# A spectral mixer and a token MLP on one core: the second product behind the up projection, PSUM read two banks at a time, and one operand loaded in K tile pairs

## The chip, the cores and the metric

The kernel runs on one core of one Trainium2 chip. The metric is the device time of one execution in microseconds (us). TensorE (PE) multiplies, VectorE (DVE) and ScalarE (ACT) prepare operands and read PSUM, SyncE (SP) issues most loads, GpSimd (POOL) issues most stores. PSUM has room for eight results of 128x512 floats, called banks here.

## The reference

```python
g = sigmoid((x * gate_w).sum(-1, keepdims=True))          # x: 2048 x 1024
a = x @ Wd_re.T ; b = x @ Wd_im.T                         # hidden DFT
A = Ws_re @ a - Ws_im @ b                                 # sequence DFT, real part
h = layernorm(x)                                          # over the 1024 channels
u = gelu(h.T @ w1 + b1)                                   # 1024 x 3584
B = (u @ w2 + b2).T                                       # 2048 x 1024
return g * A + (1 - g) * B
```

All values are 32-bit floats. The order of the two DFT products is free, so the kernel multiplies the sequence matrix first.

## The kernel before, in words

There are four matrix products, called stages: **q** (class `Fourier`: sequence transform of x), **y** (class `Mixed`: the second product, q with the hidden matrix, scaled by the gate and stored to the output), **u** (class `Up`: normalised x with w1, then gelu) and **o** (class `Down`: u with w2, added onto the output). Each stage is a product of 4x4 blocks by 4x2 blocks, done by a fixed scheme in 26 block products where the plain way has 32 (`SCHEME`). Each of the 26 multiplies a signed sum of blocks of one side by a signed sum of blocks of the other. The stationary operand (128x128 at a time) is called W and the moving one (128x512 at a time) R.

One block product runs over K tiles of 128 rows (four in q, y and u, seven in o). For every K tile both sums are made by DVE additions (`add`, `sub`), and each operand is split in two parts (`split_into`: ACT writes the high part, DVE the remainder, called lo). For each bank PE then issues three matmuls: hi·hi, hi·lo and lo·hi (lines 902 to 904). The K tiles are taken in groups (`takes`: 1, 1, 2 in q means one tile, one tile, then two together); a group does all its matmuls into the first bank, then all into the second, and so on. A product fills `nm * nn` banks: 8 in q, 4 in y, 7 in u, 4 in o.

After the last group of a product its banks are read: for each output block that the scheme names, one instruction per bank copies (L938 on ACT, L940 on DVE) or adds (L946, DVE alone) the bank into an accumulator tile (`q_c`, `y_c`, `u_c`, `o_c`). Where two products that follow each other feed nearly the same outputs, the second goes on adding in the same banks; it is then called chained, and its first matmul into a bank must wait until the reads of that bank are done.

SBUF is 51 tiles of 128x1024 and one half tile. A planner in the kernel (`Graph`) gives every task a due time from the PE order, hands out tiles and banks, and writes the order of each engine's instructions once and for all; PE's own order is the order in which the stages are built. The loads of x for the row sums, the squares and the normalisation are tasks of that planner too, with their place given by `SUMS_AT`, `SQUARES_AT` and `H_LEAD`.

Of the kernel before, what the change touches and what calls it, by code (L numbers as in the profile page):

```python
# [14 lines left out]
P = 128  # L15
S = 2048
D = 1024
# [7 lines left out]
SLOTS = {"f": 51, "h": 1, "ps": 8}  # L25
LATE = 3.0

# [112 lines left out]
Q_GAP = 8  # L140
U_ORDER = [20, 9, 8, 19, 15, 18, 1, 16, 10, 4, 21, 22, 11, 7, 3, 17, 5, 14, 23, 6, 24, 0, 13, 12, 2, 25]
# [68 lines left out]
SUMS_AT, SUMS_STEP = ("q", 12), 2.5  # L210
SQUARES_AT, SQUARES_STEP = ("y", 6), 2
H_LEAD, H_EACH = 25, 1.3
# [49 lines left out]
class Buf:  # L262
    def __init__(self, kind, name, t=None, parts=1, dtype=F32):
        self.kind, self.name, self.t, self.parts, self.dtype = kind, name, t, parts, dtype
        self.writer = [None] * parts
        self.readers = [[] for _ in range(parts)]
        self.taker = None
        self.users, self.opens = set(), False


class View:
# [8 lines left out]
    def reg(self):  # L280
        return (self.buf, self.part)

# [19 lines left out]
class Store:  # L302


    def __init__(self, slots):
        self.free = {k: [Slot(k, i) for i in range(n)] for k, n in slots.items()}
        self.part = {F32: [], F32R: []}

    def pairs(self, ahead):
        return sum((max(0, ahead[d] - len(self.part[d])) + 1) // 2 for d in self.part)  # L310

    def fits(self, b, ahead):
        if b.kind != "h":
            return len(self.free[b.kind]) > ahead[b.kind]
        if len(self.part[b.dtype]) > ahead[b.dtype]:
            return True
        return len(self.free["f"]) + len(self.free["h"]) > ahead["f"] + self.pairs(ahead)

    def take(self, b):
        if b.kind != "h":  # L320
# [3 lines left out]
        halves = self.part[b.dtype]  # L324
# [3 lines left out]
        else:  # L328
            pool = self.free["h"] or self.free["f"]
            b.slot, b.opens = (min(pool, key=lambda s: s.at), 0), True  # L330
            pool.remove(b.slot[0])
            if b.slot[0].pool == "f":
# [3 lines left out]
    def give(self, b, now):  # L336
        s, h = b.slot
        s.at = now
        if h is not None and s.pool == "f":
            s.inside[h] = False  # L340
            if s.inside[1 - h]:
                self.part[b.dtype].append(b.slot)
                return
            self.part[b.dtype].remove((s, 1 - h))
# [3 lines left out]
class Graph:  # L348
# [63 lines left out]
    def schedule(self):  # L412
        store = Store(SLOTS)
        waiting = {k: [] for k in ("f", F32, F32R, "ps")}
# [11 lines left out]
        for t in self.tasks:  # L426
# [3 lines left out]
            for b in t.need:  # L430
                insort(waiting[b.dtype if b.kind == "h" else b.kind], t)
# [14 lines left out]
        def start(t, e):  # L446
# [3 lines left out]
            for b in t.need:  # L450
                store.take(b)
                waiting[b.dtype if b.kind == "h" else b.kind].remove(t)
# [50 lines left out]
def gated_mix_kernel(  # L503
# [30 lines left out]
        "ps": (ctx.enter_context(tc.tile_pool(name="psum", bufs=1, space=bass.MemoryType.PSUM)), H),  # L534
# [138 lines left out]
    class Bilinear:  # L673
# [10 lines left out]
        behind = ()  # L684
        ahead = 3
# [723 lines left out]
```

## Time and profile before

| | |
|---|---|
| time, median of 3 runs | 1849.24 us (1849.20 to 1850.03) |
| span of the profiled execution (first to last instruction) | 1847.2 us |
| what the median has beside that span | 2.0 us |
| PE busy | 1843.0 us, 8130 matmuls |
| DVE busy | 1692.7 us, 2372 instructions |
| ACT busy | 876.2 us, 1311 instructions |
| DMA moved | 472.71 MB, mean 256 GB/s |

The profiled execution's own time is not given apart from its span. The span is cut by the stages' first matmuls: q begins at 4.06 us, y at 570.55, u at 853.43, o at 1348.47, and the last matmul ends at 1843.74. A busy PE is not by itself a PE at its peak, so the distance between the starts of matmuls is what to read, and the waits that PE had.

### The profile page before, as it was taken

Reading aid. Unit: us, or ns where it says so; the run is one execution under the profiler, and the core shown is the slowest. Engines: PE = TensorE matmul, PEld = TensorE weight load, DVE = VectorE, ACT = ScalarE, POOL = GpSimd, SP = SyncE. Lnnn points to the kernel's source line nnn. Section 1 sums busy time; section 2 is a strip of 40 time slices with the busy share of each in tenths; the row PEclk is TensorE's granted clock in tenths of the full one; section 3 lists DMA queues with packets and bytes.
Section 4 is the critical chain, followed back from the end, with each engine's and each line's share of the span. In section 5 each row is a group of like instructions: output and inputs, shape, how many; then the busy total and the mean of one; then the engine's idle time right before and its main releaser. Section 6 shows DMA issues by size and latency. Waiting matters only on the chain.

```text
span 1847.2 us, 24030 instructions
## 1 busy us (share of the span) xinstructions
PE 1843.0 (100%) x8130; PEld 1525.2 (83%) x8130; DVE 1692.7 (92%) x2372; ACT 876.2 (47%) x1311; POOL 207.2 (11%) x355
## 2 busy tenths in 40 slices
PE   9999999999999999999999999999999999999999
PEld 7888888888888888888888888888888888888887
DVE  8999679989989999999789698879999999999995
ACT  5533334534344686597343344444654534444441
POOL 0100010111021001001121000001220000001111
PEclk9999999999999999999999999999999999999999
DMA  9977377969698888988676547667899676775963
GB/s 377 368 260 270 126 280 289 349 236 376 237 333 313 303 292 273 332 312 292 219 256 241 174 136 255 225 210 247 301 365 295 193 210 208 217 215 128 301 156 69
DMA packets 189739, 472.71 MB, mean 256 GB/s; under 512 B 23152, under 2 KB 23920, under 8 KB 189616
## 3 DMA queue, kind: packets, MB, share of 16 engines
q1 hardware_dynamic: 156384, 368.40, 58.4%
q0 software_dynamic: 32944, 102.52, 16.6%
q8 instruction: 63, 1.03, 0.2%
q14 instruction: 60, 0.49, 0.1%
q10 hardware_dynamic: 288, 0.26, 0.0%
HBM read 367.29 MB, written 103.81 MB: 255 GB/s over the span
## 4 chain that ended last, share of the span: by engine, by line
PE 100%; DVE 0%; issue 0%; DVEq 0%
PE ps_q_p L902 10%; PE ps_q_p L904 10%; PE ps_q_p L903 10%; PE ps_u_p L904 9%; PE ps_u_p L902 9%; PE ps_u_p L903 9%; PE ps_o_p L902 9%; PE ps_o_p L904 9%; PE ps_o_p L903 9%; PE ps_y_p L903 5%; PE ps_y_p L904 5%; PE ps_y_p L902 5%; PE ps_q_p L1049 0%; PE ps_q_p L1026 0%; PE pw L1343 0%; DVE o_c L946 0%
## 5 line engine op out<-in xcount | busy, mean ns | idle before, releaser
L904 PE MATMUL ps_q_p<-q_p_r_hi,q_p_w_lo 128*128 128x512 f32 x728 | 283.2, 389 | 0.0
L902 PE MATMUL ps_o_p<-o_p_r,o_p_w 128*128 128x512 f32 x726 | 282.4, 389 | 0.0
L903 PE MATMUL ps_o_p<-o_p_r,o_p_w 128*128 128x512 f32 x726 | 282.4, 389 | 0.0
L904 PE MATMUL ps_o_p<-o_p_r,o_p_w 128*128 128x512 f32 x726 | 282.4, 389 | 0.0
L903 PE MATMUL ps_u_p<-u_p_r_lo,u_p_w_hi 128*128 128x512 f32 x588 | 228.7, 389 | 0.0
L902 PE MATMUL ps_q_p<-q_p_r_hi,q_p_w_lo 128*128 128x512 f32 x584 | 227.2, 389 | 0.0
L903 PE MATMUL ps_q_p<-q_p_r_lo,q_p_w_lo 128*128 128x512 f32 x584 | 227.2, 389 | 0.0
L902 PE MATMUL ps_u_p<-u_p_r_lo,u_p_w_hi 128*128 128x512 f32 x504 | 196.1, 389 | 0.0
L904 PE MATMUL ps_u_p<-u_p_r_lo,u_p_w_lo 128*128 128x512 f32 x504 | 196.1, 389 | 0.0
L599 ACT ACTIVATE q_p_r_hi<-q_R_p 128x1024 fp32r<-128x1024 f32 (+1 forms) x100 | 104.2, 1053 | 161.8 <-DVE q_R_p L569 78.7
L599 ACT ACTIVATE u_p_w_hi<-u_W_p 128x896 fp32r<-128x896 f32 x104 | 97.1, 950 | 141.1 <-DVE u_W_p L569 69.5
L904 PEld LDWEIGHTS ps_q_p<-q_p_r_hi,q_p_w_lo 128*128 128x128 f32 x728 | 136.7, 188 | 28.4
L904 PEld LDWEIGHTS ps_o_p<-o_p_r,o_p_w 128*128 128x128 f32 x726 | 136.3, 188 | 28.4
L902 PEld LDWEIGHTS ps_o_p<-o_p_r,o_p_w 128*128 128x128 f32 x726 | 136.3, 188 | 28.2
L903 PEld LDWEIGHTS ps_o_p<-o_p_r,o_p_w 128*128 128x128 f32 x726 | 136.3, 188 | 28.2
L599 ACT ACTIVATE o_p_r<-o_R_p 128x512 fp32r<-128x512 f32 x117 | 72.5, 626 | 120.9 <-PE ps_o_p L904 37.3
L903 PEld LDWEIGHTS ps_u_p<-u_p_r_lo,u_p_w_hi 128*128 128x128 f32 x588 | 110.4, 188 | 23.0
L903 PEld LDWEIGHTS ps_q_p<-q_p_r_lo,q_p_w_lo 128*128 128x128 f32 x584 | 109.6, 188 | 22.7
L902 PEld LDWEIGHTS ps_q_p<-q_p_r_hi,q_p_w_lo 128*128 128x128 f32 x584 | 109.7, 188 | 22.6
L946 DVE SCALAR_TENSOR_TENSOR q_c<-ps_q_p,q_c 128x512 f32<-128x512 f32 x168 | 110.3, 686 | 15.6 <-PE ps_q_p L904 11.5
L606 DVE TENSOR_TENSOR q_p_r_lo<-q_R_p,q_p_r_hi 128x1024 fp32r<-128x1024 f32 (+1 forms) x100 | 120.4, 1215 | 4.5 <-ACT q_p_r_hi L599 4.4
L904 PEld LDWEIGHTS ps_u_p<-u_p_r_lo,u_p_w_lo 128*128 128x128 f32 x504 | 94.6, 188 | 19.6
(322 smaller groups left out, 3989.4 us busy)
## 6 DMA issues: line engine op xcount, KB each, us to landing
q_R_p<-in_ct_dram SPq DMA_DIRECT2D x131, 512.0 KB, 7.5
u_W_p<-in_w_dram SPq DMA_DIRECT2D x120, 448.0 KB, 4.7
o_R_p<-in_w_dram SPq DMA_DIRECT2D x99, 256.0 KB, 4.7
o_R_p<-u SPq DMA_DIRECT2D x83, 256.0 KB, 5.2
q<-q_c POOLq DMA_DIRECT2D x80, 256.0 KB, 6.2
o_W_p<-in_w_dram SPq DMA_DIRECT2D x76, 256.0 KB, 4.9
q_W_p<-in_x_dram SPq DMA_DIRECT2D x75, 256.0 KB, 5.5
u<-u_c POOLq DMA_DIRECT2D x72, 256.0 KB, 4.7
```

The costliest lines, as they stand in the source:

```text
L599: g.add({"ACT": act(v.n)}, key, lambda e: nc.scalar.activation(hi.ap, v.ap, AF.Copy, scale=-1.0 if negate else 1.0), r=(v.reg,), w=(hi.reg,))
L606: nc.vector.tensor_sub(lo.ap, v.ap, hi.ap.bitcast(F32))
L902: nc.tensor.matmul(bank.ap, wh.ap[:, c], rh.ap[:, e], start=a, stop=False, skip_group_check=True)
L903: nc.tensor.matmul(bank.ap, wh.ap[:, c], rl.ap[:, e], start=False, stop=False, skip_group_check=True)
L904: nc.tensor.matmul(bank.ap, wl.ap[:, c], rh.ap[:, e], start=False, stop=b, skip_group_check=True)
L946: lambda e: nc.vector.scalar_tensor_tensor(o.ap, ps.ap, scale, o.ap, op0=ALU.mult, op1=ALU.add),
```

## The change

The change does seven things.

1. The stages are built in the order q, u, y, o (before: q, y, u, o).
2. In q, u and y PSUM is handed out as four pairs of banks, and one instruction of 1024 columns reads a pair (`banks`, `take`). In u the seventh bank of a product is still single; o keeps single banks (`together = False`). A pair is read when its second bank is complete. The loop over a product's banks now has n outside and m inside.
3. In q the stationary operand is handled in tiles of two K tiles (`Q_WIDE = "W"`: 128x1024 in place of two of 128x512), and the K tiles are taken 2, 2 (`Q_TAKES`). The first product of q alone takes 1, 1, 2.
4. The row sums start at product 4 of q (before: 12), the squares at product 12 of q (before: product 6 of y), and the normalisation begins 8 steps before use (before: 25); a step is one K tile of a product.
5. The product of x with the gate weights moves from the row sums into the normalisation, with a scratch tile of its own; the gate's last steps move to product 10 of u.
6. The planner counts at most seven earlier claims when it decides whether a task may take a tile (`RESERVE`).
7. A method `strassen`, which would do one product of q by seven half-size products, and its two helper classes are added. It is called for the products listed in `Q_INNER`, and that list is empty.

```diff
-SLOTS = {"f": 51, "h": 1, "ps": 8}
+SLOTS = {"f": 51, "h": 1, "pp": 4}
+RESERVE = 7
...
+Q_DMA = {}
+Q_INNER = ()
...
-SUMS_AT, SUMS_STEP = ("q", 12), 2.5
-SQUARES_AT, SQUARES_STEP = ("y", 6), 2
-H_LEAD, H_EACH = 25, 1.3
+SUMS_AT, SUMS_STEP = ("q", 4), 2.5
+SQUARES_AT, SQUARES_STEP = ("q", 12), 2
+GATES_AT = "u", 10
+H_LEAD, H_EACH = 8, 0.6
...
-Q_TAKES = 1, 1, 2
+Q_TAKES = 2, 2
...
-Q_WIDE, Y_WIDE, O_WIDE = "", "WR", ""
+Q_WIDE, Y_WIDE, O_WIDE = "W", "WR", ""
...
-                if not store.fits(b, {k: bisect_left(waiting[k], t) for k in waiting}):
+                if not store.fits(b, {k: min(bisect_left(waiting[k], t), RESERVE) for k in waiting}):
...
+                if j in self.inner:
+                    self.strassen(j, factor)
+                    continue
...
-            for m in range(self.nm):
-                c = slice(m * P, (m + 1) * P)
-                for n in range(self.nn):
-                    if first:
-                        self.PS[j % self.chains, m, n] = View(Buf("ps", f"ps_{self.name}_p{j}_{m}_{n}", None, 4), 0, H)
+            if first:
+                self.banks(j)
+            for n in range(self.nn):
+                for m in range(self.nm):
+                    c = slice(m * P, (m + 1) * P)
...
+        def banks(self, j):
+            every = [(m, n) for n in range(self.nn) for m in range(self.nm)]
+            for i, (m, n) in enumerate(every):
+                name = f"ps_{self.name}_p{j}_{m}_{n}"
+                if not self.together or i == len(every) - 1 and i % 2 == 0:
+                    self.PS[j % self.chains, m, n] = View(Buf("ps", name, None, 4), 0, H)
+                elif i % 2 == 0:
+                    both = Buf("pp", name, None, 2)
+                    self.PS[j % self.chains, m, n] = View(both, 0, H, 0)
+                else:
+                    self.PS[j % self.chains, m, n] = View(both, H, H, 1)
+
+        def take(self, key, j, m, n, eps):
+
+            bank, at = self.PS[j % self.chains, m, n], [(m, n)]
+            if bank.buf.kind == "pp":
+                if bank.c0 == 0:
+                    return
+                at.insert(0, (m - 1, n))
+                bank = View(bank.buf, 0, D)
...
+        def groups(self, j=None):
+            return super().groups() if j != 0 else [(0,), (1,), (2, 3)]
+
+        def unit(self, x_, k, ks):
+            return ks if x_ in self.wide and len(ks) == 2 else k
...
-        g.add({"DVE": dve(D)}, key, lambda e: nc.vector.scalar_tensor_tensor(
-            v.ap, v.ap, 1.0, GW.ap, op0=ALU.mult, op1=ALU.mult, accum_out=zg.t[:, col]),
-            r=(v.reg, GW.reg), w=(v.reg, zg))
...
+        g.add({"DVE": dve(D)}, key, lambda e: nc.vector.scalar_tensor_tensor(
+            junk.ap, v.ap, 1.0, GW.ap, op0=ALU.mult, op1=ALU.mult, accum_out=zg.t[:, col]),
+            r=(v.reg, GW.reg), w=(junk.reg, zg))
...
-    for st in (Fourier(), Mixed(), Up(), Down()):
+    for st in (Fourier(), Up(), Mixed(), Down()):
```

Three places show how instructions move. In the names, `q_R7_p1_0` is block 7 of R, loaded in product 1 for K tile 0; `_0_1` stands for a pair of K tiles; `_hi` and `_lo` are the two parts of a split; a tile that is used again keeps the name of its first user. What stands in brackets are the queues and engines that an instruction waits for.

The first place is SP at the start of q, the loads behind those of product 0. Before:

```order
L576 DMA q_R7_p1_0_277<-in_ct_dram 128x1024 [waits DMAHW3_49]
L576 DMA q_R4_p1_0_286<-in_ct_dram 128x1024 [waits DMAHW4_49]
L576 DMA q_W1_p0_3_273<-in_x_dram 128x512 [waits DMAHW5_49]
L576 DMA q_W0_p1_0_311<-in_x_dram 128x512 [waits DMAHW6_49]
L576 DMA q_R7_p1_1_315<-in_ct_dram 128x1024 [waits DMAHW7_49]
L576 DMA q_R4_p1_1_333<-in_ct_dram 128x1024 [waits DMAHW0_49]
L576 DMA q_W0_p1_0_311<-in_x_dram 128x512 [waits DMAHW1_49]
L576 DMA q_W0_p1_1_355<-in_x_dram 128x512 [waits DMAHW2_49]
L576 DMA q_R7_p1_2_361<-in_ct_dram 128x1024 [waits DMAHW3_49]
```

and now:

```order
L613 DMA q_R7_p1_0_265<-in_ct_dram 128x1024 [waits DMAHW3_49]
L613 DMA q_R4_p1_0_273<-in_ct_dram 128x1024 [waits DMAHW4_49]
L613 DMA q_R7_p1_1_279<-in_ct_dram 128x1024 [waits DMAHW5_49]
L613 DMA q_R4_p1_1_298<-in_ct_dram 128x1024 [waits DMAHW6_49]
L613 DMA q_W6_p1_0_1_302<-in_x_dram 128x512 [waits DMAHW7_49]
L613 DMA q_W6_p1_0_1_302<-in_x_dram 128x512 [waits DMAHW0_49]
L613 DMA q_W0_p1_0_1_329<-in_x_dram 128x512 [waits DMAHW1_49]
L613 DMA q_W0_p1_0_1_329<-in_x_dram 128x512 [waits DMAHW2_49]
L613 DMA q_W1_p1_0_1_344<-in_x_dram 128x512 [waits DMAHW3_49]
L613 DMA q_W1_p1_0_1_344<-in_x_dram 128x512 [waits DMAHW4_49]
```

Before, the loads of x for the first two K tiles alternated with those of R, 256 KB for each K tile and block. Now both K tiles of three blocks of x (six loads of 256 KB) stand behind the four loads of R of the first two K tiles.

The second place is DVE a little later, where the operands of product 1 are made. Before:

```order
L572 TENSOR_TENSOR q_W0_p1_0_311<-q_W1_p0_3_273,q_W0_p1_0_311 128x512 [waits DMAHW6_49,DMAHW5_49]
L940 TENSOR_SCALAR q_c5_0_410<-ps_q_p0_0_0_282 128x512 [waits PE_49]
L569 TENSOR_TENSOR q_W1_p0_0_257<-q_W0_p1_0_311,q_W1_p0_0_257 128x512 [waits DVE_49]
L606 TENSOR_TENSOR q_p1_r_0_lo_420<-q_R8_p0_0_259,q_p1_r_0_hi_400 128x1024 [waits Activation_49]
L569 TENSOR_TENSOR q_R7_p1_1_315<-q_R7_p1_1_315,q_R4_p1_1_333 128x1024 [waits DMAHW7_49,DMAHW0_49]
L604 SCALAR_TENSOR_TENSOR q_p1_w_0_lo_436<-q_W1_p0_0_257,q_p0_w_1_hi_325 128x512 [waits Activation_49]
L569 TENSOR_TENSOR q_R8_p0_1_264<-q_R7_p1_1_315,q_R8_p0_1_264 128x1024 [waits DVE_49]
L572 TENSOR_TENSOR q_W0_p1_1_355<-q_W0_p1_0_311,q_W0_p1_1_355 128x512 [waits DMAHW2_49,DMAHW1_49]
L940 TENSOR_SCALAR q_c5_4_457<-ps_q_p0_2_0_293 128x512 [waits PE_49]
```

and now:

```order
L606 TENSOR_TENSOR q_R7_p1_0_265<-q_R7_p1_0_265,q_R4_p1_0_273 128x1024 [waits DMAHW4_49,DMAHW3_49]
L606 TENSOR_TENSOR q_R8_p0_0_247<-q_R7_p1_0_265,q_R8_p0_0_247 128x1024 [waits DVE_49]
L606 TENSOR_TENSOR q_R7_p1_1_279<-q_R7_p1_1_279,q_R4_p1_1_298 128x1024 [waits DMAHW6_49,DMAHW5_49]
L643 TENSOR_TENSOR q_p1_r_0_lo_392<-q_R8_p0_0_247,q_p1_r_0_hi_379 128x1024 [waits Activation_49]
L606 TENSOR_TENSOR q_R8_p0_1_252<-q_R7_p1_1_279,q_R8_p0_1_252 128x1024 [waits DVE_49]
L609 TENSOR_TENSOR q_W0_p1_0_1_329<-q_W6_p1_0_1_302,q_W0_p1_0_1_329 128x1024 [waits DMAHW2_49,DMAHW7_49,DMAHW1_49,DMAHW0_49]
L643 TENSOR_TENSOR q_p2_w_0_1_lo_430<-q_W6_p1_0_1_302,q_p2_w_0_1_hi_402 128x1024 [waits Activation_49]
L606 TENSOR_TENSOR q_W1_p1_0_1_344<-q_W0_p1_0_1_329,q_W1_p1_0_1_344 128x1024 [waits DMAHW4_49,DMAHW3_49,DVE_49]
L643 TENSOR_TENSOR q_p1_r_1_lo_447<-q_R8_p0_1_252,q_p1_r_1_hi_418 128x1024 [waits Activation_49]
L606 TENSOR_TENSOR q_R7_p1_2_367<-q_R7_p1_2_367,q_R4_p1_2_371 128x1024 [waits DMAHW6_49,DMAHW5_49]
L641 SCALAR_TENSOR_TENSOR q_p1_w_0_1_lo_462<-q_W1_p1_0_1_344,q_p1_w_0_1_hi_452 128x1024 [waits Activation_49]
```

Before, the operands of K tile 0 (down to the remainder `q_p_w_lo`, line 604) came ahead of most of those of K tile 1. Now the W sums and splits are 1024 wide and hold both K tiles, and the remainder of W for product 1 (line 641) is the eleventh instruction of the piece. Its high part is written by ACT after the addition of line 606 into `q_W1_p1_0_1`.

The third place is DVE in y, at the end of product 9, on which product 10 is chained. Before:

```order
L606 TENSOR_TENSOR y_p12_r_1_5658<-q_W0_p1_3_424,y_p12_r_1_5658 128x512 [waits Activation_49]
L946 SCALAR_TENSOR_TENSOR y_c1_0_5092<-ps_y_p9_0_0_5603,y_c1_0_5092 128x512 [waits PE_49]
L946 SCALAR_TENSOR_TENSOR y_c7_0_5575<-ps_y_p9_0_0_5603,y_c7_0_5575 128x512
L606 TENSOR_TENSOR y_p12_w_1_5679<-y_R4_p4_1_4752,y_p12_w_1_5679 128x512 [waits Activation_49]
L946 SCALAR_TENSOR_TENSOR y_c1_0_5092<-ps_y_p9_1_0_5619,y_c1_0_5092 128x512 [waits PE_49]
L946 SCALAR_TENSOR_TENSOR y_c7_0_5575<-ps_y_p9_1_0_5619,y_c7_0_5575 128x512
L946 SCALAR_TENSOR_TENSOR y_c1_2_5112<-ps_y_p9_2_0_5632,y_c1_2_5112 128x512 [waits PE_49]
L946 SCALAR_TENSOR_TENSOR y_c7_2_5598<-ps_y_p9_2_0_5632,y_c7_2_5598 128x512
L946 SCALAR_TENSOR_TENSOR y_c1_2_5112<-ps_y_p9_3_0_5646,y_c1_2_5112 128x512 [waits PE_49]
L946 SCALAR_TENSOR_TENSOR y_c7_2_5598<-ps_y_p9_3_0_5646,y_c7_2_5598 128x512
```

and now:

```order
L609 TENSOR_TENSOR y_W10_p6_2_3_8658<-y_W10_p6_2_3_8658,y_W10_p11_2_3_9125 128x1024 [waits DMAHW7_49,DMAHW0_49]
L1016 SCALAR_TENSOR_TENSOR y_c1_0_8753<-ps_y_p9_0_0_9211,y_c1_0_8753 128x1024 [waits PE_49]
L1016 SCALAR_TENSOR_TENSOR y_c7_0_9200<-ps_y_p9_0_0_9211,y_c7_0_9200 128x1024
L1016 SCALAR_TENSOR_TENSOR y_c1_2_8775<-ps_y_p9_2_0_9238,y_c1_2_8775 128x1024 [waits PE_49]
L1016 SCALAR_TENSOR_TENSOR y_c7_2_9218<-ps_y_p9_2_0_9238,y_c7_2_9218 128x1024
L643 TENSOR_TENSOR y_p11_r_2_3_lo_9321<-y_R4_p10_2_3_9082,y_p11_r_2_3_hi_9171 128x1024 [waits DMASW5_49]
L641 SCALAR_TENSOR_TENSOR y_p11_w_2_3_lo_9329<-y_W10_p6_2_3_8658,y_p11_w_2_3_hi_9294 128x1024 [waits Activation_49]
```

Before, the eight reads were one for each of four banks and two outputs. Now there are four reads, each of a pair of banks, two for each pair.

More of the change, by code (lines that the diff above doesn't have):

```diff
@@ L413, in schedule @@
         store = Store(SLOTS)
-        waiting = {k: [] for k in ("f", F32, F32R, "ps")}
+        waiting = {k: [] for k in ("f", F32, F32R, "ps", "pp")}
         left, users = {}, {}
@@ L684, in gated_mix_kernel @@
         behind = ()
+        halved = ()
+        together = True
         ahead = 3
@@ L694, in __init__ @@
             small = [r[1] for r in rows]
-            self.again = {j: s for j in range(1, len(rows)) for s in (1, -1) if small[j] == [s * c for c in small[j - 1]]}
+            self.inner = [j for j, r in enumerate(order) if r in self.halved]
+            self.again = {j: s for j in range(1, len(rows)) for s in (1, -1)
+                          if small[j] == [s * c for c in small[j - 1]] and not {j, j - 1} & {*self.inner}}
             self.kept = {}
@@ L711, in __init__ @@
                 opposite = sum(a != -b for a, b in zip(w, v))
-                go_on = min(same, opposite) < sum(a != 0 for a in w)
+                go_on = min(same, opposite) < sum(a != 0 for a in w) and i + n not in self.inner
                 self.chained.append(go_on)
@@ new lines, in take @@
+        def take(self, key, j, m, n, eps):
[5 more added lines that the diff above has]
+                bank = View(bank.buf, 0, D)
+            for q, coef in self.reads[j]:
+                b = self.perm[0][q // 2] * 2 + self.perm[2][q % 2]
+                new, back = (b, m, n) not in self.C, self.back(b, j)
+                if new:
+                    for one in at:
+                        self.C[(b, *one)] = self.c_slots(f"{self.name}_c{b}", b, *one)
+                os = [self.C[(b, *one)] for one in at]
+                o = os[0] if len(at) == 1 else View(os[0].buf, 0, D)
+                if new and back:
+                    for one, part in zip(at, os):
+                        self.bring(key - self.ahead, b, *one, part)
+                if new and not back:
+                    self.copy(key, b, m, n, o, bank, eps * coef)
+                else:
+                    self.accumulate(key, b, m, n, o, bank, eps * coef)
+                if j in self.ends[b]:
+                    for one in at:
+                        self.finish(key + 1, b, *one, self.C.pop((b, *one)), j)
@@ L1032, in matmuls @@
                 return super().matmuls(j, ks, ops, eps)
+            self.banks(0)
             for n in range(2):
[L1034 to L1035 removed]
                 for i, (w, r) in enumerate(((wh, rh), (wl, rh), (wh, rl))):
```

191 lines of the change are left out of this document (146 added, 45 removed).

## The prediction

> **What bounds the kernel now.** I read the page's first two parts, then the waits of PE, then the stages one by one.
>
> ```profile
> span 1847.2 us, 24030 instructions
> PE 1843.0 (100%) x8130; PEld 1525.2 (83%) x8130; DVE 1692.7 (92%) x2372; ACT 876.2 (47%) x1311; POOL 207.2 (11%) x355
> ...
> PEclk9999999999999999999999999999999999999999
> DMA  9977377969698888988676547667899676775963
> ...
> PE 100%; DVE 0%; issue 0%; DVEq 0%
> ```
>
> ```profile
> engine line waited for: us in total, times, longest us
> PE pw L1343 <- PEq L1396: 0.8, 1, 0.8
> ```
>
> The second answer is the whole list of what PE waited for: 0.8 us once, before its warm-up. The chain of waits is PE from end to end. Cut at the stages' borders (q, y, u, o):
>
> ```profile
> 0.00:4.35 4.35, 3.57 (x9) 1.34 (x10) 0.59 (x2) 1.86 (x3) 0.20 (x4) 1.00 0.56 155
> 4.35:570.40 566.05, 566.05 (x2500) 469.06 (x2500) 511.49 (x650) 229.20 (x319) 65.60 (x116) 1.00 0.81 294
> 570.40:853.30 282.90, 282.90 (x1250) 234.33 (x1249) 274.94 (x381) 204.22 (x295) 27.63 (x51) 1.00 0.86 305
> 853.30:1348.60 495.30, 495.30 (x2187) 410.27 (x2186) 435.17 (x575) 224.54 (x323) 64.44 (x119) 1.00 0.67 229
> 1348.60:1843.80 495.20, 495.14 (x2191) 410.17 (x2189) 470.07 (x766) 216.39 (x374) 49.33 (x65) 1.00 0.71 212
> ```
>
> Each row gives the stretch and its length, then busy time and count of PE, weight loads, DVE, ACT and POOL, the granted clock, the DMA share and GB/s. In every stage the length over the matmuls is 0.226 us (566.05/2500, 495.30/2187), at clock 1.00: PE never slows. So the span is about 4.1 us of start, 8100 matmuls at 0.227 us, and 3.4 us after the last matmul; the median has 2.0 us beside it. Only the number of matmuls, their pitch, the two ends, or new stalls can move the time. DVE is behind PE by little (512 of 566, 275 of 283, 435 of 495, 470 of 495 us), but behind.
>
> **What the change leaves alone.** The order of instructions has 8130 matmuls in both programs, since the list of products for `strassen` is empty. Shapes and operand types are the same, so the pitch is. Start-up up to the first matmul and the halved last banks are the same code. A gain could come only from the 7.5 us of both ends, and nothing in the diff touches them: 0.
>
> **Work taken from DVE.** Two durations carry this: rows of several instructions in the order of time (start, length of the row, instruction, count) give the pitch.
>
> ```profile
> 26.74 4.62 DVE L569 TENSOR_TENSOR q_R_p<-q_R_p,q_R_p 128x1024 f32<-128x1024 f32 x4
> ...
> 677.27 3.67 DVE L946 SCALAR_TENSOR_TENSOR y_c<-ps_y_p,y_c 128x512 f32<-128x512 f32 x6
> ```
>
> Six reads of one bank take 3.67 us: 0.60 each, 0.68 for the last with its end. Four of 1024 columns in SBUF take 4.62: 1.13 each, 1.22 for the last. A read of a pair is not in this trace. I take 1.13, by that row; its bounds are 1.13 and twice a single read, 1.20, as the PSUM rows cost what SBUF rows of the same width cost. A pair instead of two banks thus saves 0.07 us. DVE's order is 306 instructions shorter (2358 to 2052). At 0.07 each that is some 20 us, all on an engine for which PE never waited: 0 on the end, bounds 0 and 0. The product with the gate weights (16 x 1.13 = 18 us) moves from q into the end of q and the start of u; u has 60 us of idle DVE to hide it. Without that cover it would cost at most 18 us less the 54 us idle in q: still nothing.
>
> **Loads.** The stretch in which the loads were densest:
>
> ```profile
> 10.00:20.00 10.00, 10.00 (x46) 8.28 (x45) 9.01 (x11) 5.79 (x9) 0.00 (x0) 1.00 1.04 407
> ```
>
> Squares and normalised rows (32 loads of 512 KB, 17 MB) now fall in q: 17 MB over 566 us adds 30 GB/s to 294. That is far under the 407 that were moved here, so they fit: 0. The early ones in y and u go away.
>
> **Stage order.** y no longer follows the stage that makes its input, and o no longer follows u; both gaps grow to a whole stage. u needs only x and the row statistics. What SP, POOL and ACT do is put elsewhere, not added to: 0. If DVE comes late to a border, see the rivals.
>
> **Term 1: product 1 of q starts late.** Before, its first group was one K tile; now it is two, with W in pairs, so the operands of K tile 1 are due 5.4 us earlier. What was there:
>
> ```profile
> 14.99 2.48 DVE L569 TENSOR_TENSOR q_R_p<-q_R_p,q_R_p 128x1024 f32<-128x1024 f32 x2 [0.50 <-DMA q_R_p<-in_ct_dram]
> ...
> 26.55 0.39 PE L902 MATMUL ps_q_p<-q_p_r_hi,q_p_w_hi 128*128 128x512 f32 x1
> 26.77 0.39 PE L903 MATMUL ps_q_p<-q_p_r_lo,q_p_w_hi 128*128 128x512 f32 x1
> 27.00 0.39 PE L904 MATMUL ps_q_p<-q_p_r_hi,q_p_w_lo 128*128 128x512 f32 x1
> ...
> 31.99 0.39 PE L902 MATMUL ps_q_p<-q_p_r_hi,q_p_w_lo 128*128 128x512 f32 x1
> ```
>
> At 407 GB/s 512 KB take 1.29 us. The DVE row waits for block 7 and 4 of K tile 0, landed at 14.9; the same bytes stand ahead of them now. Behind come R for K tile 1 (1 MB: 17.5), then three blocks of x of 512 KB each: 18.8, 20.0, 21.3. DVE goes through the eleven instructions shown of its new order: the first at 14.95; the second waits for the end of the first (16.2); the third for its load (17.5); then 18.65, 19.8, and, no load being late any more, 20.9, 22.05, 23.2, 24.3, 25.45, and the last, the remainder of W, from 26.6 to 27.8. The third matmul wanted it at 27.00. PE stalls **0.9 us** with the signal. Bounds: 0 if loads come a little faster, 2 if one instruction of 1.13 more gets in between. The high part of W comes from ACT after the eighth, at about 26.2, in time. The second group then starts at 26.55 + 0.9 + 10.9 = 38.3; its remainder of W is the ninth instruction after the eleven, 36.8 to 38.0, wanted at 38.8: just in time. Later products have the slack of before.
>
> **Term 2: reads of pairs in y.** y has four banks, so a chained product comes back to a bank after 4 x 6 matmuls. Before, the first bank of product 9's last group was free for reading from 675.27 (six matmuls from 673.91) to 679.35:
>
> ```profile
> 673.91 0.39 PE L902 MATMUL ps_y_p<-y_p_r_hi,y_p_w_hi 128*128 128x512 f32 x1
> ...
> 675.27 0.39 PE L902 MATMUL ps_y_p<-y_p_r_hi,y_p_w_hi 128*128 128x512 f32 x1
> ...
> 679.35 0.39 PE L902 MATMUL ps_y_p<-y_p_r,y_p_w 128*128 128x512 f32 x1
> ...
> 675.47 1.29 DVE L946 SCALAR_TENSOR_TENSOR y_c<-ps_y_p,y_c 128x512 f32<-128x512 f32 x2 [0.79 <-PE ps_y_p L904]
> ...
> 818.07 0.39 PE L902 MATMUL ps_y_p<-y_p_r_hi,y_p_w_hi 128*128 128x512 f32 x1
> ...
> 816.90 1.29 DVE L946 SCALAR_TENSOR_TENSOR y_c<-ps_y_p,y_c 128x512 f32<-128x512 f32 x2
> 818.11 1.22 DVE L606 TENSOR_TENSOR y_p_r_lo<-y_R_p,y_p_r_hi 128x1024 fp32r<-128x1024 f32 x1
> 819.25 3.67 DVE L946 SCALAR_TENSOR_TENSOR y_c<-ps_y_p,y_c 128x512 f32<-128x512 f32 x6
> ```
>
> The window was 4.08 us; two reads began 0.20 after it opened and ended at 676.76, 2.6 us early. A pair is complete only after twelve matmuls and is wanted at the same moment: the window is 2.72 us. One read takes 0.20 + 1.22 and leaves 1.3. Two take 0.20 + 1.13 + 1.22 = 2.55 and leave 0.17. In the changed order two reads of each pair stand before a chained product after products 9, 22 and 24, and after 11 one by ACT and one by DVE, in turn: four places, eight pairs. In thirteen more one read stands. To this comes what DVE is still busy with. The rows bound it: 0 as at 675.47; or, at product 22, 1.0 (its second bank was done 0.20 after 818.07, when the third began, and its reads began at 819.25, behind another instruction). In the middle, 0.5, the first pair of each place stalls 0.5 - 0.17 = 0.33, and the second gains from that stall but for an instruction between them: 0.4 a place, **1.5 us** for four. Bounds: 0, and 8 x (1.0 - 0.17) = 6.6. The thirteen single ones have 1.3 us against 1.0: 0. Behind a waiting read on DVE stand the splits of later products; at 675.47 DVE had waited 0.79 us for PE, so it is ahead of need there and can afford it.
>
> The same reading for q gives a window of 8 x 1.36 - 2.72 = 8.2 us, for u 7 x 1.36 - 2.72 = 6.8 against three reads of 3.7; o keeps single banks. 0 for all three.
>
> **Sum.** The profiled execution: 1847.2 + 0.9 + 1.5 = 1849.6 us of span; with the 2.0 beside it, **1851.6 us**, that is 2.4 more than the median.
>
> **The rivals.**
> A: *pairs stall PE all through y.* Place: all seventeen chained starts, 34 pairs. If DVE, at 275 of 283 us, is on average a whole 1.13 us instruction and a short one of 0.60 late, a single read misses by 1.73 - 1.3 = 0.43 a place and a double by 1.56, with the second pair in the lee of the first: 13 x 0.43 + 4 x 1.56 = 12 us, with term 1 1862; half of it is likelier, 1856. It decides from 0.17 us a place on (3.7 - 0.9 over 17). For it: a DVE so full. Against it: of the reads in the rows above the latest came 1.0 after its bank was done. The Trainium skill, "Perfetto Trace Analysis", section "Matmuls", asks that groups rotate through banks so that reading one overlaps the next; four pairs are half as many units to rotate as eight banks, which is this rival. In this trace, with eight, PE never waited; with four, no run here shows it yet.
> B: *nothing stalls*; both terms are slack again: 1849.2.
> C: *DVE comes late at a border*, at the start of u (18 us of gate products and eight rows to normalise) or of y (DVE at 275 of 283 us before). Five instructions of 1.13 us: 1855. Against: DVE is idle 54 us of q and 60 of u ahead of them, in which it can work ahead.
> D: *faster by more than 3.7 us*: half of both ends would have to vanish; 1845 or less.
> E: *the recursion runs*: each such product would save 12 of 96 matmuls, 2.7 us, 1846.5 with one. The equal count of matmuls excludes it.
>
> **Chances.** This kernel's runs can tell 0.2% (3.7 us) from no change. The forecast 0.52, own range 1849.6 to 1853.5; A 0.24; B 0.15; C 0.07; D 0.02; E 0. Same: nearly all of the forecast and B, 0.63. Slower: A, C and the forecast's upper edge, 0.35. Faster 0.02. The range runs from 1849.0 (most of B) to 1857.0 (half of A).
>
> **What would show it.** Term 1: a wait of PE for DVE's remainder of W (line 641 of the new file) near 27 us, about 0.9 long, and none in the next products. Term 2: PE waits for DVE's read of `ps_y` at four places, some tenths each. Wrong, if PE's waits list a DMA, if stalls stand at most chained starts of y (A), if PE waits for splits at a stage's first products (C), or if the pitch is not 0.227. DVE must fall to about 1670 us.

## The result: 1.3% slower, and the profile after

The changed kernel takes 1874.13 us (median of 4 runs, 1873.28 to 1874.89), the kernel before beside it 1849.63 us (4 runs). The ratio is 1.0132, with a 95% interval of 1.0117 to 1.0146: 24.5 us slower, clear of noise, and far above the upper end of the forecast range (1857.0).

The span grew from 1847.2 to 1871.9 us. The first view to read is the busy time of PE in each stage, cut at the stages' first matmuls. Columns: stretch, length, PE busy (matmuls), granted clock, DMA share, GB/s. Before, in the order q, y, u, o:

```profile
4.06:570.55 566.49, 566.49 (x2502) 1.00 0.81 294
570.55:853.43 282.88, 282.88 (x1250) 1.00 0.86 305
853.43:1348.46 495.03, 495.03 (x2185) 1.00 0.67 229
1348.46:1843.86 495.40, 495.28 (x2191) 1.00 0.71 212
```

After, in the order q, u, y, o:

```profile
4.01:571.70 567.69, 566.70 (x2502) 1.00 0.85 312
571.70:1066.74 495.04, 495.04 (x2186) 1.00 0.67 231
1066.74:1353.09 286.35, 284.78 (x1249) 1.00 0.80 272
1353.09:1867.50 514.41, 500.98 (x2191) 1.00 0.67 200
```

q is 1.2 us longer, u the same, y 3.5 longer and **o 19.0 longer**. With 1.1 us more behind the last matmul (1867.5 to 1871.9, against 1843.86 to 1847.2) that makes the whole 24.7 us of the span. The clock is 1.00 throughout and the matmuls are as many as before, so PE waited. The list of PE's waits after the change says for whom (columns: who waited, for whom, us in total, times, longest):

```profile
PE ps_o_p L948 <- DVE o_c L1016: 11.3, 11, 1.7
PE ps_o_p L948 <- ACT o_c L1401: 1.6, 2, 0.8
PE ps_y_p L948 <- DVE y_c L1016: 1.5, 3, 0.7
PE ps_q_p L950 <- DVE q_p_w_lo L641: 1.0, 1, 1.0
PE pw L1537 <- PEq L1590: 0.8, 1, 0.8
PE ps_o_p L948 <- DVE o_c L1403: 0.4, 1, 0.4
```

The third and the fourth row are the two terms of the forecast. The first, second and last are new: 13.3 us in o, the stage that "keeps single banks". All three of these are matmuls that want to write a bank and wait for a reader of PSUM.

**One such place, step by step.** Product 5 of o ends and product 6, which is not chained, begins. PE's instructions there after the change: the last of the six matmuls of product 5's first, second and fourth bank, then the first bank of product 6 and the start of its second (start, duration, and in brackets the idle time before and who ended it):

```profile
1465.87 0.39 PE L950 MATMUL ps_o_p<-o_p_r,o_p_w 128*128 128x512 f32 x1
...
1467.23 0.39 PE L950 MATMUL ps_o_p<-o_p_r,o_p_w 128*128 128x512 f32 x1
...
1469.95 0.39 PE L950 MATMUL ps_o_p<-o_p_r,o_p_w 128*128 128x512 f32 x1
1472.01 0.50 PE L948 MATMUL ps_o_p<-o_p_r,o_p_w 128*128 128x512 f32 x1 [1.67 <-DVE o_c L1016]
1472.35 0.39 PE L949 MATMUL ps_o_p<-o_p_r,o_p_w 128*128 128x512 f32 x1
...
1473.27 0.40 PE L950 MATMUL ps_o_p<-o_p_r,o_p_w 128*128 128x512 f32 x1
1475.23 0.50 PE L948 MATMUL ps_o_p<-o_p_r,o_p_w 128*128 128x512 f32 x1 [1.56 <-DVE o_c L1016]
```

ACT's copies of product 5's four banks, after the change:

```profile
1467.72 0.69 ACT L1401 ACTIVATE o_c<-ps_o_p,hgate 128x512 f32<-128x512 f32 x1 [4.30 <-PE ps_o_p L950]
1469.22 0.69 ACT L1401 ACTIVATE o_c<-ps_o_p,hgate 128x512 f32<-128x512 f32 x1 [0.82 <-DVE o_c L1016]
1470.44 0.69 ACT L1401 ACTIVATE o_c<-ps_o_p,hgate 128x512 f32<-128x512 f32 x1 [0.52 <-PE ps_o_p L950]
1473.71 0.69 ACT L1401 ACTIVATE o_c<-ps_o_p,hgate 128x512 f32<-128x512 f32 x1 [2.58 <-PE ps_o_p L950]
```

And DVE's additions from the first, third and fourth of them, after the change:

```profile
1468.44 0.75 DVE L1016 SCALAR_TENSOR_TENSOR o_c<-ps_o_p,ngate,o_c 128x512 f32<-128x512 f32 x1 [0.64 <-ACT o_c L1401]
...
1471.21 0.75 DVE L1016 SCALAR_TENSOR_TENSOR o_c<-ps_o_p,ngate,o_c 128x512 f32<-128x512 f32 x1
...
1474.43 0.75 DVE L1016 SCALAR_TENSOR_TENSOR o_c<-ps_o_p,ngate,o_c 128x512 f32<-128x512 f32 x1 [1.87 <-ACT o_c L1401]
```

Four things are seen. ACT's first copy begins at 1467.72, when the *second* bank is complete (1467.23 + 0.39); the first, which it reads, was complete at 1466.26 (1465.87 + 0.39). Product 6 cannot start at 1470.18, one pitch behind product 5's last matmul: it starts at 1472.01, just when DVE has read the *third* bank of product 5 (1471.21 + 0.75). Its second six matmuls start at 1475.23, just when DVE has read the *fourth* (1474.43 + 0.75). And ACT's copy of the fourth bank, complete since 1470.34, waits 2.58 us for PE: it runs at 1473.71, behind the six matmuls that product 6 has put in another bank.

The order of PE's instructions in the changed kernel has the reason in the tile's name. `ps_o_p4_2_0` is a tile of two banks, opened for bank 2 of product 4; product 5, chained to product 4, ends in it:

```
L950 MATMUL ps_o_p4_2_0_11499<-o_p5_r_6_11534,o_p5_w_6_11540 128x512
L948 MATMUL ps_o_p4_2_0_11499<-o_p6_r_0_11563,o_p6_w_0_11528 128x512 [waits DVE_49]
```

Before, the same two rows are

```
L904 MATMUL ps_o_p4_3_0_11891<-o_p5_r_6_11967,o_p5_w_6_11974 128x512
L902 MATMUL ps_o_p6_0_0_12175<-o_p6_r_0_12002,o_p6_w_0_11929 128x512 [waits Activation_49]
```

There product 6 followed one pitch behind product 5, and DVE read the last bank of product 5 only after that. PE (end of product 5, start of product 6) and DVE before the change:

```profile
1462.48 0.39 PE L904 MATMUL ps_o_p<-o_p_r,o_p_w 128*128 128x512 f32 x1
1462.70 0.39 PE L902 MATMUL ps_o_p<-o_p_r,o_p_w 128*128 128x512 f32 x1
```

```profile
1463.82 0.75 DVE L946 SCALAR_TENSOR_TENSOR o_c<-ps_o_p,ngate,o_c 128x512 f32<-128x512 f32 x1
```

So a product that was given a bank of its own before is given the two banks that its predecessor has just filled. That is one half of it, called **the choice of the bank** below: the planner's `Store.take`, which hands out a single bank as half of a two-bank tile, takes a free half of a tile in use before it opens a tile that is wholly free. The other half is **the shared tile**: in the waits of this program a read of one bank is held up by a write to the other bank of its tile, and a write by the other bank's read (ACT's copies at 1467.72 and 1473.71 are such reads). The two readers take turns as well: ACT's second copy starts at 1469.22, just when DVE has read the first bank (1468.44 + 0.75). Before, where each bank was a tile of its own, no wait of PE for a reader is listed at all.

### The profile page after: what moved, and what is told of

Its sections match the earlier page's. It is cut to its first block, busy times and chain, and to the rows that moved or that the text cites. A ratio compares the mean times of both kernels' runs of the same rounds, so it can differ in the third digit from the quotient of the medians.

```text
span 1871.9 us, 23569 instructions
## 1 busy us (share of the span) xinstructions
PE 1850.7 (99%) x8130; PEld 1521.9 (81%) x8130; DVE 1671.0 (89%) x2066; ACT 869.8 (46%) x1203; POOL 200.7 (11%) x346
## 5 line engine op out<-in xcount | busy, mean ns | idle before, releaser
L950 PE MATMUL ps_q_p<-q_p_r_hi,q_p_w_lo 128*128 128x512 f32 x816 | 317.5, 389 | 1.0 <-DVE q_p_w_lo L641 1.0
L949 PE MATMUL ps_q_p<-q_p_r_lo,q_p_w_hi 128*128 128x512 f32 x816 | 317.4, 389 | 0.0
L948 PE MATMUL ps_q_p<-q_p_r_hi,q_p_w_hi 128*128 128x512 f32 x816 | 317.4, 389 | 0.0
L948 PE MATMUL ps_o_p<-o_p_r,o_p_w 128*128 128x512 f32 x726 | 284.7, 392 | 13.3 <-DVE o_c L1016 11.3
L949 PE MATMUL ps_u_p<-u_p_r_lo,u_p_w_hi 128*128 128x512 f32 x518 | 201.5, 389 | 0.0
L950 PEld LDWEIGHTS ps_q_p<-q_p_r_hi,q_p_w_lo 128*128 128x128 f32 x816 | 153.2, 188 | 33.1 <-DVE q_p_w_lo L641 1.4
L949 PEld LDWEIGHTS ps_q_p<-q_p_r_lo,q_p_w_hi 128*128 128x128 f32 x816 | 153.2, 188 | 31.9
L948 PEld LDWEIGHTS ps_q_p<-q_p_r_hi,q_p_w_hi 128*128 128x128 f32 x816 | 153.2, 188 | 31.8
L948 PE MATMUL ps_u_p<-u_p_r_hi,u_p_w_hi 128*128 128x512 f32 x385 | 149.8, 389 | 0.0
L950 PE MATMUL ps_u_p<-u_p_r_hi,u_p_w_lo 128*128 128x512 f32 x385 | 149.8, 389 | 0.0
L948 PE MATMUL ps_u_p<-u_p_r_lo,u_p_w_hi 128*128 128x512 f32 x343 | 133.4, 389 | 0.0
L1016 DVE SCALAR_TENSOR_TENSOR q_c<-ps_q_p,q_c 128x1024 f32<-128x1024 f32 x84 | 101.2, 1221 | 31.4 <-PE ps_q_p L950 24.3
```

Of the source, the lines that this page charges most:

```text
L948: nc.tensor.matmul(bank.ap, wh.ap[:, c], rh.ap[:, e], start=a, stop=False, skip_group_check=True)
L949: nc.tensor.matmul(bank.ap, wh.ap[:, c], rl.ap[:, e], start=False, stop=False, skip_group_check=True)
L950: nc.tensor.matmul(bank.ap, wl.ap[:, c], rh.ap[:, e], start=False, stop=b, skip_group_check=True)
L1016: lambda e: nc.vector.scalar_tensor_tensor(o.ap, ps.ap, scale, o.ap, op0=ALU.mult, op1=ALU.add),
```

## The experiments

The theory to test was: the two-bank PSUM tile costs the time, by the choice of the bank and by the shared tile. Its first rival was the stage order, which the forecast had put at 0: o now follows y, in which DVE is busy 99% of the time, where it used to follow u, in which it is idle 60 us, so DVE could simply come late into o.

**All banks single again.** Everything else stays changed.

```diff
-SLOTS = {"f": 51, "h": 1, "pp": 4}
+SLOTS = {"f": 51, "h": 1, "pp": 8}
...
-        "pp": (... space=bass.MemoryType.PSUM)), D),
+        "pp": (... space=bass.MemoryType.PSUM)), H),
...
-        together = True
+        together = False
...
```

> The changed kernel with eight PSUM tiles of one bank each in place of four tiles of two, and every read 512 wide again; stage order, K tile pairs and all else as changed. Theory 1 (the two-bank tile is the cause: in the fourth stage a fresh product is given the banks that were just finished, and reads and writes of one bank wait for the other bank of its tile): PE's 13.3 us of waits in the fourth stage and 1.5 us in the third vanish, the tail after the last matmul falls from 4.8 to about 3.7 us, the wait of 1.0 near 27 us stays; span 1847.2 + 1.2 = 1848.4, time about 1850.4 us. Rival (stage order: DVE comes out of the third stage with no lead, so it is late in the fourth): the fourth stage still waits over 10 us, time 1865 or more.

Measured: 1852.01 us (10 runs), ratio 1.0012 (1.0002 to 1.0021). Its list of PE's waits:

```profile
PE ps_q_p L950 <- DVE q_p_w_lo L641: 0.9, 1, 0.9
...
```

All waits in y and o are gone, and with them 22 of the 24.5 us. The time is 1.6 us above the expected 1850.4, 0.7 of it in the profiled span (1849.1 against 1848.4). The rival falls: stage order, moved loads, gate and the planner's cap are all in this kernel.

**The old stage order, with two-bank tiles.** The counter-test:

```diff
-    for st in (Fourier(), Up(), Mixed(), Down()):
+    for st in (Fourier(), Mixed(), Up(), Down()):
...
-SUMS_AT, SUMS_STEP = ("q", 4), 2.5
-SQUARES_AT, SQUARES_STEP = ("q", 12), 2
-H_LEAD, H_EACH = 8, 0.6
+SUMS_AT, SUMS_STEP = ("q", 12), 2.5
+SQUARES_AT, SQUARES_STEP = ("y", 6), 2
+H_LEAD, H_EACH = 25, 1.3
```

(The gate product goes back to the row sums, since y needs the gates before u is built.)

> The changed kernel with the old order of the stages (transform, second product, up, down) and the old places of the row sums, squares and gates; two-bank tiles, K tile pairs and the cap on slot reservations stay. Theory 1: the fourth stage stalls as before this edit, 13 to 19 us, and the third product stage a few: 1868 to 1876 us. Rival (stage order is the cause): the fourth stage follows one in which DVE is idle 60 us, so it no longer waits: about 1855 us.

Measured: 1874.83 us, ratio 1.0137 (1.0122 to 1.0152). The last stage, o, of this run:

```profile
1354.14:1868.20 514.06, 501.47 (x2191) 1.00 0.68 205
```

o is as long as in the changed kernel (514.1 against 514.4 us), although it follows u. The stage order has no part in it that can be seen.

**The choice of the bank alone.** A single bank may use the second half of a tile only while that half has not been used since the tile was opened; otherwise the tile that has been free longest is opened. In o of this run, the two banks of a tile are then always of one product.

```diff
         halves = self.part[b.lane]
+        if b.kind == "ps" and self.free["pp"]:
+            halves = [x for x in halves if x[0].new]
         if halves:
             b.slot = min(halves, key=lambda x: x[0].at)
-            halves.remove(b.slot)
+            self.part[b.lane].remove(b.slot)
+            b.slot[0].new = False
...
             pool.remove(b.slot[0])
+            b.slot[0].new = True
```

> The changed kernel, but a single bank may take the second half of a two-bank tile only from the tile that its own product has just opened; else it opens the free tile that has been idle longest. Fresh products then start on tiles that nobody reads, while the tiles still have two banks. Theory 1: the eleven stalls of fresh products 3, 6, 9, 12, 15, 16 of the fourth stage (15.4 of the 18.4 us that its matmul gaps hold over the pitch) vanish, the small ones at chained products (3 us), those of the third stage (3.5) and the longer tail (1.1) stay: about 1858 us. Rival (stage order, DVE late): the stalls move to other places, time 1868 to 1874.

Measured: 1860.64 us, ratio 1.0061 (1.0046 to 1.0076). Its last stage, and PE's waits there:

```profile
1354.65:1855.30 500.65, 498.34 (x2191) 1.00 0.69 206
```

```profile
PE ps_o_p L952 <- DVE o_c L1020: 1.7, 3, 1.3
PE ps_o_p L952 <- DVE o_c L1407: 0.4, 1, 0.4
```

o falls from 514.4 to 500.65 us: the choice of the bank was worth 13.8 us. That is 1.6 less than the 15.4 expected, and 5.3 us stay over the 495.4 of before. The waits listed stand at the start of chained products, the longest (1.3 us) at that of product 7. q is 1.6 us longer than in the changed kernel too (569.25 us), by waits of PE at its start.

**The shared tile too.** Now a single bank opens a free tile whenever there is one, so the four banks of a product of o lie in four tiles:

```diff
-        if halves:
+        if halves and not (b.kind == "ps" and self.free["pp"]):
```

> The changed kernel, but a single bank opens a free two-bank tile as long as there is one, so that the four banks of a product of the fourth stage lie in four tiles. Theory 1: each of them is read and written with the window that single banks had (4.08 us less the reads), so all of the 18.4 us of gaps in the fourth stage and the 1.1 of the tail go; the 1.3 of the first stage and 3.5 of the third stay: about 1854 us. If only the choice of the tile mattered and not that two banks share one, this would equal the run in which tiles are kept in pairs. Rival (stage order): 1868 to 1874.

Measured: 1853.93 us (9 runs), ratio 1.0026 (1.0016 to 1.0036). Its last stage, o:

```profile
1352.95:1848.30 495.35, 495.27 (x2191) 1.00 0.70 208
```

o is back at 495.35 us, with nothing waited for. If only the choice of the bank counted, this would have equalled the run before; the 5.3 us between them are the shared tile. It is not a lack of banks either: by the addresses in the program PE writes only the first half of each tile in o here, so o does with four of the eight banks. ACT's copies after product 5 of o in this kernel show the difference to the rows above:

```profile
1463.37 0.69 ACT L1401 ACTIVATE o_c<-ps_o_p,hgate 128x512 f32<-128x512 f32 x1 [2.94 <-PE ps_o_p L950]
1464.67 0.69 ACT L1401 ACTIVATE o_c<-ps_o_p,hgate 128x512 f32<-128x512 f32 x1 [0.61 <-PE ps_o_p L950]
1466.09 0.69 ACT L1401 ACTIVATE o_c<-ps_o_p,hgate 128x512 f32<-128x512 f32 x1 [0.73 <-PE ps_o_p L950]
1467.39 0.69 ACT L1401 ACTIVATE o_c<-ps_o_p,hgate 128x512 f32<-128x512 f32 x1 [0.61 <-PE ps_o_p L950]
```

They are 1.3 to 1.4 us apart, the six matmuls of a bank; none waits for DVE, and none is late.

**The same in y.** The spread banks in the third stage as well, which makes its reads 512 wide:

```diff
 class Mixed(Bilinear):
+    together = False
```

> The kernel that spreads the four banks of a product over four tiles (1853.9), now in the third stage too, whose reads become 512 wide; the first two stages keep pair reads. Theory 2 (a pair is only complete after twelve matmuls, so the window of a chained start is 2.72 us): with the window of 4.08 back, the third stage's 3.0 us of gaps go although DVE has some 2 us more to do there: about 1850.5 us. Rival (DVE is too full in the third stage whatever the reads): the stalls stay, 1854.

Measured: 1851.24 us, ratio 1.0010 (1.0000 to 1.0019). y takes 282.87 us, as before the change, although DVE has more instructions there (384 against 350); it is not too full for them:

```profile
1067.11:1349.98 282.87, 282.87 (x1249) 1.00 0.80 277
```

**512-wide reads on shared tiles, in y.** The edit of `Mixed` from the last run, on the kernel of the run on the choice of the bank; it asks whether the wide read or the shared tile costs y its window.

> The kernel that keeps a product's banks in pairs (1860.6), with the third stage's reads 512 wide instead of 1024. Theory 1 (a read of one bank waits for the last matmul of the other bank of its tile, and a write for the other bank's read): 512 wide reads do not bring the window back, the third stage keeps 3 us or more of gaps, 1860 to 1863 us. Rival (it is the length of the 1024 wide read): the gaps of the third stage go, 1857.

Measured: 1858.23 us, ratio 1.0047 (1.0032 to 1.0062). PE's waits in y in this run:

```profile
PE ps_y_p L952 <- DVE y_c L1020: 2.0, 2, 1.5
...
```

y takes 286.6 us, as with wide reads (286.3), and waits 2.0 us, no less than the 1.5. The waits have moved, though. After products 9 and 24 they are gone from the list, and the longest, 1.48 us, is new, at the second bank of product 6. The tiles hold other pairs in this run: y begins in a half tile that was left over, so the second and third bank of a product share a tile, and the first lies beside the last one of an earlier product. PE, and DVE's reads of product 5's second, third and fourth bank (one instruction each, the last two in one row):

```profile
1135.33 0.50 PE L952 MATMUL ps_y_p<-y_p_r,y_p_w 128*128 128x512 f32 x1 [1.48 <-DVE y_c L1020]
```

```profile
1132.26 0.68 DVE L1020 SCALAR_TENSOR_TENSOR y_c<-ps_y_p,y_c 128x512 f32<-128x512 f32 x1
...
1134.60 1.28 DVE L1020 SCALAR_TENSOR_TENSOR y_c<-ps_y_p,y_c 128x512 f32<-128x512 f32 x2
```

The second bank itself had been read by 1132.94 (1132.26 + 0.68). PE went on at 1135.33, when the first of the last two reads, that of the third bank, was done (1134.60 + 0.68). So here the shared tile alone held PE up, without a wide read. What each would cost at the three places of the changed kernel, the run does not tell apart, since the pairs differ. The time came out 2 us below what the theory said, and nearer to the rival's 1857, since o and q lost less in this run; the rows, not the time, decide between the two.

**The first groups of q.** On the kernel with single banks, the old K tile groups:

```diff
-Q_TAKES = 2, 2
+Q_TAKES = 1, 1, 2
-Q_WIDE, Y_WIDE, O_WIDE = "W", "WR", ""
+Q_WIDE, Y_WIDE, O_WIDE = "", "WR", ""
```

> The one-bank kernel of the run before (1852.0), with the old K tile groups of the first stage too (one, one, two tiles, the stationary operand one K tile at a time). Theory (term 1: the wider first group of product 1 makes DVE's remainder late): the wait of 0.9 us near 27 us goes and the first stage takes 566.3 instead of 567.4 us: about 1850.8 us. Rival (it is the cap on slot reservations or the loads moved into the first stage that delay the start): the wait stays, 1852.

Measured: 1850.08 us, ratio 1.0004 (0.9994 to 1.0013), no change that can be told. q takes what it took before:

```profile
4.06:570.61 566.55, 566.55 (x2502) 1.00 0.85 312
```

What is left of the change in this kernel (stage order, moved loads and gate, the cap) costs and brings nothing that can be told.

**A version that beats both?** PE is busy from the first matmul to the last, so only fewer matmuls could do much. The changed kernel carries the recursive product, unused. It was switched on for a few products of q on the kernel with banks spread in y and o (1851.24 us).

```diff
-Q_INNER = ()
+Q_INNER = (3,24,)
...
-            add(step, q12, q22, q21)
+            c21 = View(Buf("f", f"{name}_c21", None, 2), 0, D)
+            plain_copy(step, c21, q21, 1.0)
+            add(step, q12, q22, c21)
...
```

> The kernel of this call that spreads the banks in the third and fourth stage, with the recursive form switched on for two products of the first stage (rows 3 and 24 of the scheme; its two additions of one PSUM pair to another get a copy to SBUF ahead of them). Each such product has 84 matmuls instead of 96: 24 x 0.2267 = 5.4 us less on PE. Theory (PE is the bound and DVE has 80 us idle in the first stage): about 1845.5 us. Rival (the copies and additions between the sevenths stand on PE's path): each product loses 2 to 5 us in waits for DVE, 1848 to 1855.

> As the run with the recursion on for rows 3 and 24, but for rows 24 and 0, which come tenth and thirteenth in the first stage instead of fourth and tenth. In the run before, the fourth product lost 5.1 us to waits for DVE between 91 and 107 us, where DVE was 94 per cent busy, and the tenth lost none. Theory: late products keep the whole 2.7 us each, 1851.2 - 5.4 = 1845.8 us. Rival (a recursive product costs what it saves wherever it stands): 1850 to 1852.

> Three recursive products (rows 24, 0 and 1). DVE was busy 483 us of the first stage without any, and 515 with two, that is 16 more for each: 531 of about 560 us. Theory: 1851.2 - 8.2 = 1843.0 us. Rival (DVE too full): 1846 or more.

> Four (rows 24, 0, 12 and 1): DVE 547 of about 557 us. Theory: 1851.2 - 10.9 = 1840.3 us if DVE can be used to the end; at 98 per cent it is the edge. Rival (above some 95 per cent each instruction more on DVE costs PE its own time): no better than three, 1843 to 1850.

> Five (rows 24, 0, 9, 12 and 1): DVE would need 563 us of about 554: it becomes the bound. Theory: 9 us or more of waits for DVE come back, 1847 us or more, worse than four. Rival (work that DVE shares with ACT moves over): 1837.6.

Measured, in this order: 1851.13 us (ratio 1.0012, 1.0003 to 1.0022), 1853.98 (1.0025, 1.0015 to 1.0034), 1852.09 (1.0015, 1.0005 to 1.0024), 1859.48 (1.0051, 1.0035 to 1.0068) and 1864.98 (1.0086, 1.0071 to 1.0101). None is faster than before, and the theory that late products keep their 2.7 us fell with the second run. There the product of row 24 lost nothing, but the one of row 0 lost some 7 us between 283 and 303 us. DVE in and behind that place, in the run with rows 24 and 0 (columns after the length: PE, PEld, DVE, ACT, POOL busy, clock, DMA share, GB/s):

```profile
283.00:287.40 4.40, 2.29 (x7) 0.80 (x5) 4.40 (x6) 3.01 (x4) 0.00 (x0) 1.00 1.02 413
287.40:291.40 4.00, 3.90 (x10) 2.76 (x11) 4.00 (x5) 3.94 (x9) 0.00 (x0) 0.57 1.03 400
290.00:340.00 50.00, 47.97 (x207) 38.69 (x206) 50.00 (x45) 30.42 (x42) 7.48 (x14) 0.99 0.95 349
```

DVE is busy 4.40 of 4.40 us and 50.00 of 50.00: the stage's mean (510 of 571 us) hid that DVE has no room in this stretch, and a recursive product needs 16 us of it. One product in the right place would give 2.7 us, 0.15%, less than can be told here; it was not tried.

## Why the prediction was wrong

**What failed is one sentence**: "o keeps single banks. 0 for all three." The three are q, u and o. For q and u the 0 is right. For o it is wrong by 19.0 us of the 22.5 that separate the forecast (1851.6) from the result. o's *reads* are single, as the code says (`together = False`), but its *banks* are halves of the two-bank tiles that the other stages need. The sentence took the reads for the banks. (The other 3.4 us are 2.0 of y, 1.1 of the program's end and 0.3 of q.) Of the 19.0, the choice of the bank is 13.8 (514.4 to 500.65) and the shared tile 5.3 (500.65 to 495.35). At the program's end the shared tile takes 0.6 of another 1.1: the last four reads of DVE end at 1868.69, 1.3 us behind the last matmul (1867.38); before it was 0.65 (1844.39 and 1843.74), and it is 0.66 again in the run with the four banks of o in four tiles. PE and DVE at the end of the changed kernel:

```profile
1865.79 1.59 PE L1430 MATMUL ps_o_p<-o_p_r,o_p_w 128*128 128x256 f32 x12
1865.99 2.70 DVE L1016 SCALAR_TENSOR_TENSOR o_c<-ps_o_p,ngate,o_c 128x512 f32<-128x512 f32 x4 [1.97 <-PE ps_o_p L950]
```

It could have been read ahead of the run. The rows of PE's order name the tile, and `ps_o_p4_2_0` stands there for the last bank of one product and the first of the next. The prediction read the order only at the start of q and at the reads of y, since it took the change to leave o alone.

**Term 1 was right in mechanism, place and size of the wait**: 0.9 us forecast near 27 us, 0.99 measured at 28.02, and the instruction waited for begins at 26.74 where 26.6 was worked out. PE and DVE after the change:

```profile
28.02 0.50 PE L950 MATMUL ps_q_p<-q_p_r_hi,q_p_w_lo 128*128 128x512 f32 x1 [0.99 <-DVE q_p_w_lo L641]
```

```profile
26.74 1.22 DVE L641 SCALAR_TENSOR_TENSOR q_p_w_lo<-q_W_p,q_p_w_hi 128x1024 fp32r<-128x1024 f32 x1
```

q grew by 1.2 us, about this wait and the 0.27 that the next paragraph finds on top of one. On the kernel with single banks, the old groups take it away again (q falls from 567.57 to 566.55 us).

**Term 2 was right in place and in the waits, too small in what they cost.** Four places of some tenths each were forecast, after products 9, 11, 22 and 24, 1.5 us in all; PE waits after 9, 11 and 24, and the sum is 1.5. That three longer waits add up to what four were to make is luck:

```profile
1176.58 0.47 PE L948 MATMUL ps_y_p<-y_p_r,y_p_w 128*128 128x512 f32 x1 [0.46 <-DVE y_c L1016]
...
1201.97 0.50 PE L948 MATMUL ps_y_p<-y_p_r,y_p_w 128*128 128x512 f32 x1 [0.66 <-DVE y_c L1016]
...
1342.09 0.47 PE L948 MATMUL ps_y_p<-y_p_r,y_p_w 128*128 128x512 f32 x1 [0.35 <-DVE y_c L1016]
```

Yet y grew by 3.5 us, not 1.5. A wait is counted from the modelled end of the matmul before (0.39 us after its start), while the pitch is 0.227: the listed wait leaves out 0.16 us. Behind it the next matmul is late as well: 0.34 us after the one at 1472.01 in the rows above, 0.11 over the pitch. So each stall costs its wait and about 0.27 (three of them 2.3 us), and the other 1.2 us are delays too short for the list. The reason given (a pair is complete only after twelve matmuls) is part of it at most: y loses as much with 512-wide reads on shared tiles, and nothing with them on tiles of their own. How the three waits divide between the two is open.

**The rest.** DVE fell to 1671 us, as forecast, and that brought nothing, as forecast; the loads in q and the stage order cost 0. Rival A, that pairs make PE stall, came nearest, with a chance of 0.24. But its stalls were those of a late DVE at the chained products of y; its price of 7 to 13 us was for a stage that lost 3.5, and neither o nor the choice of the bank was in it. Rival C, DVE late at a border, looked at the start of u and of y; the list of PE's waits after the change has none for the operands of u, y or o, and o is as long when it follows u, so no border mattered. The rule cited with rival A, from the Trainium skill, "Perfetto Trace Analysis", section "Matmuls" (independent matmul groups should rotate through the banks, so that reading one overlaps the next), agrees with these runs: product 6 of o is such an independent group, and sent back to the bank just filled it stood 1.67 and 1.56 us. The list of what would make the prediction wrong had no row for o either.

## What to carry to other kernels

When a pool changes its unit, go through every user of that pool, also those whose own code is untouched: ask which buffer the next user is given, and what else lies in the same tile, and read both from the names in the order of instructions. An engine that never waits gains nothing from a less busy neighbour, so such a change can only lose, and its price lies in the windows that it narrows. A listed wait of PE is less than it costs: set the lengths of the stages against each other, not the waits.

## What was not expected of the hardware

A stall can cost the clock. In the changed kernel none of the stalls, up to 1.7 us, is seen to lower the granted clock: around the two longest, from 1471 to 1479 us, it is 1.00, with PE busy 5.42 of 8.00 us. In the run with four recursive products PE stood still for 5.7 us, and came back at about half the clock for 4 us (columns as in the last table of this kind):

```profile
426.00:430.20 4.20, 0.00 (x0) 0.00 (x0) 4.20 (x5) 0.00 (x0) 2.08 (x4) 0.64 1.03 413
430.20:434.20 4.00, 3.97 (x10) 3.16 (x11) 4.00 (x4) 2.64 (x3) 1.94 (x4) 0.52 1.02 417
434.20:438.00 3.80, 3.80 (x18) 3.13 (x17) 3.80 (x4) 0.53 (x1) 0.21 (x1) 1.00 1.03 419
```

10 matmuls in 4.0 us, where 18 fill 3.8 at full clock: some 1.7 us on top of the 5.7 (10 matmuls at the pitch of 0.227 take 2.3). In the run with rows 24 and 0, four stalls of 0.4 to 0.7 us, from 283.6 to 287.5 us, went ahead of the same (PE busy 2.29 of 4.40 us, then the clock 0.57 for 4 us; the rows are above). In the run with rows 3 and 24, three such stalls from 104.3 to 106.9 us (PE busy 3.78 of 5.20 us) did not: the clock is 1.00 in the 3.8 us behind them. The Trainium skill, "TensorE: Matmul & The Clock Gate", section "What's actually happening", has the clock fall to a half after an idle window of about 3.4 us. The stall of 5.7 us agrees; the four short ones, with PE busy half of 4.4 us, do not fit a window that must be idle throughout. What decides for short stalls is not shown here.
